# Linear attention with experts on one core: the first four chunks' loads in single pieces, the first gates in halves, one product moved to GpSimd, seven warm products fewer

## The chip, the core and the metric

The kernel runs on one core of a Trainium2 chip. Five engines work side by side, each through its own list of instructions in order: TensorE (matrix products, into PSUM), VectorE, ScalarE, GpSimd and SyncE, which here issues the loads. Sixteen DMA engines move the data. The metric is the device time of one execution in microseconds; lower is better.

## The reference

A gated linear attention feeds a mixture of eight experts, of which each token takes one. There are 4 batches, 8 heads of 48 and 768 steps, so 3072 tokens of 384 values.

```python
f = 1.0 / (1.0 + np.exp(-f_logit))
for t in range(S):
    state = f[:, :, t, :, None] * state + np.einsum('bhd,bhe->bhde', k[:, :, t], v[:, :, t])
    y[:, :, t] = np.einsum('bhd,bhde->bhe', q[:, :, t], state)
...
logits = x @ w_gate
e_idx = np.argmax(logits, axis=1)
eom = 1.0 / (1.0 + np.exp(-(x @ w_output_gate)))
for e in range(E):
    h = np.maximum(x[mask] @ w1[e], 0.0)
    out[mask] = gate_w[mask, None] * eom[mask, e, None] * (h @ w2[e])
```

## The kernel before

**Tiles.** A chunk is 128 steps of one batch, all heads: 6 chunks a batch, 24 in all, numbered t = 0 to 23 in `order` (line 462). q, k and f are laid out as 128 partitions (two heads of 48, padded to 64) by 4 groups of heads (`NP`) by 768 steps; v has the steps of a chunk on the partitions.

**What a chunk needs first** (`prep`, lines 209 to 249). ScalarE turns f into gates with a sigmoid: `s` the start values (128x4) and the first element of `p`, `f` the other 127 steps of four groups (128x508) into PSUM. VectorE forms the running product `p` with one scan over all 511 elements (`scan_p`; the four groups are cut from each other by a zero at the end of each group in the gates), then a reciprocal and the scan backwards (`scan_i`). q is multiplied by `p` (`mul_q`, GpSimd) and k by `i` (`mul_k`, on VectorE for chunks 1 and 2 and from chunk 22 on, else on GpSimd). ScalarE keeps the last column (`ends`).

**The chunk itself.** TensorE forms 16 score products (`qk`, line 266) into two PSUM tiles, of which there are two in all, so that chunk t+1 writes where chunk t was read. ScalarE copies the scores out (line 271) and GpSimd masks them (line 272); from chunk 2 on VectorE masks one half from PSUM (line 277). TensorE then turns k (line 285), turns the output of two chunks before (`x_tr`, line 347, after ScalarE's copies of line 339), multiplies q with the state (line 328) and the scores with v (line 332), and adds to the state (line 301).

**The order.** Each engine's order is that of the program text (`chain`, line 1340). The loop over t (line 510) writes chunk t's products beside the preparation of chunk t+2, and the start values of chunk t+3 from t = 3 on (line 564). Ahead of the loop stand chunks 0 and 1 (lines 499 to 501) and the gates of chunk 2 (line 502).

**The loads.** SyncE issues them in order (lines 465 to 471), `load(b, cuts)` with pieces (which tensors, first chunk, chunk behind the last). One chunk of q, k or f is 256 KiB, in rows of 512 B; two chunks in one load have rows of 1024 B. Batch 0 is followed by batch 1 in pieces of two chunks.

**Warm products.** `warm_up` runs products of zeros whose results nobody reads: `WARM` = 18 at the start (line 77), 5 that wait for chunk 0's `scan_p` and 4 for its `scan_i` (lines 503 and 504).

**After the attention** the tokens are routed, scattered by expert, and the eight experts' two layers run on TensorE to the end; none of that is touched.

Of the kernel before, what the change touches and what calls it, by code (L numbers as in the profile page):

```python
# [8 lines left out]
F32 = mybir.dt.float32  # L9
# [4 lines left out]
AF = mybir.ActivationFunctionType  # L14
ALU = mybir.AluOpType
# [6 lines left out]
C = 128  # L22
NCH = S // C
NP = H // 2
CAPS = (480, 448, 432, 416, 400, 400, 384, 376)
WARM = 18
TS = 128
NT = 4
SLOTS = NT * TS
# [18 lines left out]
T_VEC = 22  # L48
# [11 lines left out]
def behind_of(tc, d, other):  # L60

    tc.add_manual_dep(d.ins, other.ins.name,
                      mybir.DependencyInfo(mybir.DependencyClass.Sync, mybir.DependencyReason.DATA), reason="order")


def warm_up(nc, k, ps, n, tc=None, after=None):
    for i in range(n):
        d = nc.tensor.matmul(ps, k.warm[:, 0:128], k.warm, start=True, stop=True)
        if after is not None and i == 0:
            behind_of(tc, d, after)  # L70


def make_consts(nc, k, pool, prep, ps, ends):

    k.warm = pool.tile([128, 512], BF16, name="warm")
    nc.vector.memset(k.warm, 0.0)
    warm_up(nc, k, ps, WARM)

# [22 lines left out]
def more_consts(nc, pool, k, r):  # L101

    k.upper = pool.tile([128, 128], BF16, name="upper")
    nc.gpsimd.memset(k.upper, 1.0)
    nc.gpsimd.affine_select(out=k.upper, in_=k.upper, pattern=[[1, 128]], compare_op=ALU.is_gt,
                            fill=0.0, base=0, channel_multiplier=-1)
    k.ones = pool.tile([128, 128], BF16, name="ones")
    nc.gpsimd.memset(k.ones, 1.0)

    k.first = pool.tile([128, E], F32, name="first")  # L110
    nc.gpsimd.iota(out=k.first, pattern=[[-1, E]], base=E, channel_multiplier=0, allow_small_or_imprecise_dtypes=True)
    k.first_key = pool.tile([128, E], F32, name="first_key")
    nc.gpsimd.iota(out=k.first_key, pattern=[[-1 - E * N, E]], base=E, channel_multiplier=0,
                   allow_small_or_imprecise_dtypes=True)

    k.num = pool.tile([128, E], F32, name="num")
    nc.gpsimd.iota(out=k.num, pattern=[[1, E]], base=0, channel_multiplier=0, allow_small_or_imprecise_dtypes=True)
    k.slot0 = pool.tile([128, E], F32, name="slot0")
    nc.gpsimd.iota(out=k.slot0, pattern=[[N, E]], base=0, channel_multiplier=0, allow_small_or_imprecise_dtypes=True)
    k.place = pool.tile([128, E, E], F32, name="place")  # L120
    nc.gpsimd.iota(out=k.place, pattern=[[1, E], [0, E]], base=0, channel_multiplier=0,
                   allow_small_or_imprecise_dtypes=True)

    nc.gpsimd.iota(out=r.ohb[:, 0, 0, :], pattern=[[N // 128, E]], base=0, channel_multiplier=0,
                   allow_small_or_imprecise_dtypes=True)
# [16 lines left out]
def attention(ctx, tc, nc, k, kpool, rt, q01, k01, f01, q23, k23, f23, v, wg, xs_dram, r, ex):  # L142
# [11 lines left out]
    pf = done_sb.enter_context(tc.tile_pool(name="at_pre", bufs=4, side="right"))  # L154
# [4 lines left out]
    f_t = [pe.tile([128, NP, S], F32, name=f"f_t{i}") for i in range(2)]  # L159
# [10 lines left out]
    f_ps = psB.tile([128, NP, C], F32, name="f_ps")  # L170
# [13 lines left out]
    def load(b, cuts, after=None):  # L184
        i = b % 2

        def issue(out, in_):
            d = nc.sync.dma_start(out=out, in_=in_)
            if after is not None:
                behind_of(tc, d, after)  # L190
        if b not in v_t:
            v_t[b] = vp.tile([128, NCH, H * 64], F32, name="v_t")
        src = {"f": (f_t[i], f01, f23), "k": (k_t[i], k01, k23), "q": (q_t[i], q01, q23)}
        for what, c0, c1 in cuts:
            sl = slice(c0 * C, c1 * C)
            for w in what:
                if w == "v":
                    issue(out=v_t[b][:, c0:c1, :], in_=v[b, sl].rearrange("(c p) h e -> p c (h e)", p=C))
                    continue
                t, first, rest = src[w]  # L200
                if b < 2:
                    issue(out=t[:, :, sl], in_=first[b, :, :, sl].rearrange("g p s -> p g s"))
                    continue
                for g in (0, 2):
                    for par in range(2):
                        issue(out=t[64 * par:64 * par + D, g:g + 2, sl],
                              in_=rest[b - 2, 2 * g + par:2 * g + par + 3:2, :, sl].rearrange("g d s -> d g s"))

    def prep(ti):
        b, c = order[ti]  # L210
        i, sl, z = b % 2, slice(c * C, (c + 1) * C), ti % 2
        flat = lambda a: a.rearrange("p g t -> p (g t)")
        eng = nc.vector if ti in (1, 2) or ti >= T_VEC else nc.gpsimd
        d = {}

        def s():

            nc.scalar.activation(out=k.start_p[z][:, :, 0:1], in_=f_t[i][:, :, c * C:c * C + 1], func=AF.Sigmoid)  # L218
            d["p"] = pf.tile([128, NP, C], F32, name="p", bufs=3)
            nc.scalar.copy(out=d["p"][:, 0, 0:1], in_=k.start_p[z][:, 0, 0:1])  # L220

        def f():

            d["f"] = {1: f_y, 2: f_x}.get(ti, f_ps)
            nc.scalar.activation(out=d["f"][:, :, 0:C - 1], in_=f_t[i][:, :, c * C + 1:c * C + C], func=AF.Sigmoid)

        def scan_p():

            n, sp = NP * C, flat(k.start_p[z])
            d["scan_p"] = nc.vector.tensor_tensor_scan(out=flat(d["p"])[:, 1:n], data0=flat(d["f"])[:, 0:n - 1], data1=sp[:, 1:n],  # L230
                                         initial=sp[:, 0:1], op0=ALU.mult, op1=ALU.max)

        def scan_i():

            nc.vector.reciprocal(out=k.start_i[z][:, :, C - 1:C], in_=d["p"][:, :, C - 1:C])
            d["i"] = pf.tile([128, NP, C], F32, name="i", bufs=3)
            d["scan_i"] = nc.vector.tensor_tensor_scan(out=flat(d["i"])[:, ::-1], data0=flat(d["f"])[:, ::-1],  # L237
                                         data1=flat(k.start_i[z])[:, ::-1], initial=0.0, op0=ALU.mult, op1=ALU.max)

        def mul_k():  # L240
            d["mul_k"] = eng.tensor_tensor(out=k_t[i][:, :, sl], in0=k_t[i][:, :, sl], in1=d["i"], op=ALU.mult)

        def mul_q():
            nc.gpsimd.tensor_tensor(out=q_t[i][:, :, sl], in0=q_t[i][:, :, sl], in1=d["p"], op=ALU.mult)  # L244

        def ends():
            nc.scalar.copy(out=r.pend[:, ti * NP:ti * NP + NP].unsqueeze(2), in_=d["p"][:, :, C - 1:C])

        return locals()
# [4 lines left out]
    def hot(t):  # L254
        return 0 <= t < len(order)
# [206 lines left out]
    order = [(b, c) for b in range(B) for c in range(NCH)]  # L462
    last = len(order) - 1
    pre_of = [prep(t) for t in range(len(order))]
    load(0, [("f", 0, 1), ("q", 0, 2), ("f", 1, 2), ("k", 0, 2), ("f", 2, 4), ("v", 0, 1), ("qk", 2, 4)])
    nc.sync.dma_start(out=turn[:, 0::2, 2 * D:XW], in_=wg[:, 0::2, 0:2 * E])
    for i in range(2):
        nc.sync.dma_start(out=turn[64 * i:64 * i + 64, 1::2, 2 * D:XW],
                          in_=wg[64 - 64 * i:128 - 64 * i, 1::2, 0:2 * E])
    load(0, [("v", 1, 4), ("fkqv", 4, 6)])  # L470
    load(1, [("fkqv", 0, 2), ("fkqv", 2, 4), ("fkqv", 4, 6)])
    ex.empty_rows()

    def pre(t, *names):
        if hot(t):
            for nm in names:
                if nm not in done[t]:
                    done[t].add(nm)
                    pre_of[t][nm]()
# [13 lines left out]
    for g in range(2):  # L493
        for j in range(2):
            r0 = 64 * (j ^ g)
            nc.gpsimd.tensor_copy(out=turn[:, g::2, D * j:D * j + D],
                                  in_=k.ident[:, r0:r0 + D].unsqueeze(1).broadcast_to([128, 2, D]))
    more_consts(nc, kpool, k, r)
    for names in (("f", "s"), ("scan_p", "mul_q", "ends", "scan_i", "mul_k")):
        pre(0, *names)  # L500
        pre(1, *names)
    pre(2, "s", "f")
    for name, n in (("scan_p", 5), ("scan_i", 4)):
        warm_up(nc, k, one, n, tc, pre_of[0]["d"][name])

    ends, t0 = {}, 0
# [3 lines left out]
    for t in range(last + 1):  # L510
# [84 lines left out]
        if t in share:  # L595
            b, what, c = share[t]
# [823 lines left out]
```

## Time and profile before

| | us |
|---|---|
| median of 3 runs | 336.77 (335.91 to 337.01) |
| the profiled execution | 335.95 |
| its span, first to last instruction | 334.2 |
| TensorE busy in the span | 326.7 |
| first score products of chunk 0 | 9.68 |
| first score products of chunk 2 | 15.09 |

The profile is of one execution; its times count from its first instruction. A row of a timeline gives the start, the duration, the engine, the line, the operation with the tile written and the tiles read, and in brackets how long the engine had been idle and what ended that. "x16" means that 16 instructions of one kind stand together in the row.

### The profile page before, as it was taken

The numbers are of one execution on the slowest core, as the hardware profiler recorded it, in microseconds if no ns is written. First come the engines' busy times: TensorE is split into PE (matmuls) and PEld (weight loads), VectorE is DVE, ScalarE is ACT, GpSimd is POOL, SyncE is SP. The second block draws the span as 40 slices with busy tenths as digits, with TensorE's granted clock in tenths as the row PEclk, the third lists the DMA queues.
The fourth block names the chain that finished last, engine by engine and source line by source line (L and its number), as shares of the span: only waits on it lengthen the run. The fifth ranks groups of instructions, "written<-read, shape, count | busy, mean of one in ns | idle before, by whom it ended". The sixth has DMA issues, their size and how long they took to land. (4 is left out here: it accounts for less than half of the span.)

```text
span 334.2 us, 8698 instructions
## 1 busy us (share of the span) xinstructions
PE 326.7 (98%) x3002; PEld 307.9 (92%) x3002; DVE 262.6 (79%) x538; ACT 182.5 (55%) x434; POOL 144.4 (43%) x185
## 2 busy tenths in 40 slices
PE   8999999999999999999999999999999999999993
PEld 3788888889898899999999999999999999999992
DVE  6999999898999677586885985985986886989700
ACT  4777776877775762565642543452552662553610
POOL 7778789999988883031000005003104103203251
PEclk9999999999999999999999999999999999999999
DMA  7999999966666834999999399699699699593531
GB/s 241 348 355 360 303 227 275 251 180 203 195 220 216 263 140 158 239 183 348 130 301 216 54 294 316 125 263 341 137 250 328 140 234 329 156 252 115 141 121 46
DMA packets 85715, 75.15 MB, mean 225 GB/s; under 512 B 40661, under 2 KB 80278, under 8 KB 85648
## 3 DMA queue, kind: packets, MB, share of 16 engines
q1 hardware_dynamic: 82352, 64.61, 71.2%
q0 software_dynamic: 3296, 9.65, 8.2%
q8 instruction: 42, 0.69, 0.9%
q14 instruction: 25, 0.20, 0.2%
HBM read 57.83 MB, written 16.81 MB: 223 GB/s over the span
## 5 line engine op out<-in xcount | busy, mean ns | idle before, releaser
L1041 POOL DMA_INDIRECT out<-yr,dst x23 | 23.6, 1025 | 129.4 <-DMA yr<-yd 95.1
L947 PE MATMUL h_ps<-xl,w1h 128*128 128x224 f32 (+7 forms) x192 | 63.2, 329 | 0.0
L947 PE MATMUL h_ps<-xh,w1l 128*128 128x224 f32 (+7 forms) x192 | 63.1, 329 | 0.0
L947 PE MATMUL h_ps<-xh,w1h 128*128 128x224 f32 (+7 forms) x192 | 62.9, 328 | 0.0
L958 ACT ACTIVATE hh<-h_ps 128x400 fp32r<-128x400 f32 (+7 forms) x70 | 33.8, 483 | 52.1 <-PE h_ps L947 51.1
L959 DVE SCALAR_TENSOR_TENSOR hl<-h_ps,hh 128x400 fp32r<-128x400 f32 (+7 forms) x70 | 37.5, 537 | 22.8 <-ACT hh L958 22.3
L979 PE MATMUL y_ps<-hh,w2l 128*128 128x424 f32 (+5 forms) x144 | 49.0, 341 | 0.0
L979 PE MATMUL y_ps<-hl,w2h 128*128 128x424 f32 (+5 forms) x144 | 48.9, 340 | 0.0
L979 PE MATMUL y_ps<-hh,w2h 128*128 128x424 f32 (+5 forms) x144 | 48.9, 339 | 0.0
L947 PEld LDWEIGHTS h_ps<-xh,w1h 128*128 128x128 f32 x192 | 36.1, 188 | 0.2
L947 PEld LDWEIGHTS h_ps<-xh,w1l 128*128 128x128 f32 x192 | 36.1, 188 | 0.1
L947 PEld LDWEIGHTS h_ps<-xl,w1h 128*128 128x128 f32 x192 | 36.1, 188 | 0.1
L244 POOL TENSOR_TENSOR q_t<-q_t,p 128x512 f32<-128x512 f32 x24 | 30.6, 1275 | 3.4 <-DMA q_t<-in_q 1.6
L741 DVE TENSOR_TENSOR w2l<-w2r,w2h 128x768 fp32r<-128x768 f32 x31 | 29.6, 956 | 2.5 <-ACT w2h L740 0.7
L230 DVE TENSOR_TENSOR_SCAN p<-f_ps,start_p 128x511 f32<-128x511 f32 x22 | 28.0, 1274 | 2.8 <-ACT start_p L218 1.2
L266 PE MATMUL a_ps<-q_t,k_t 64*128 64x128 f32 x384 | 28.3, 285 | 0.2 <-ACT at L271 0.2
L237 DVE TENSOR_TENSOR_SCAN i<-f_ps,start_i 128x512 f32<-128x512 f32 x22 | 26.9, 1223 | 0.8
L741 DVE TENSOR_TENSOR w1l<-w1r,w1h 128x768 fp32r<-128x768 f32 x28 | 26.6, 952 | 0.9 <-ACT w1h L740 0.2
L364 POOL DMA_INDIRECT xs_dram<-xn,slot x24 | 24.1, 1006 | 7.1 <-issue 3.6
L979 PEld LDWEIGHTS y_ps<-hh,w2h 128*128 128x128 f32 x144 | 27.0, 188 | 0.1
L979 PEld LDWEIGHTS y_ps<-hl,w2h 128*128 128x128 f32 x144 | 27.0, 188 | 0.1
L979 PEld LDWEIGHTS y_ps<-hh,w2l 128*128 128x128 f32 x144 | 27.0, 188 | 0.1
(201 smaller groups left out, 736.4 us busy)
## 6 DMA issues: line engine op xcount, KB each, us to landing
w1r<-in_w SPq DMA_DIRECT2D x32, 384.0 KB, 6.2
w2r<-in_w SPq DMA_DIRECT2D x32, 384.0 KB, 5.6
v_t<-in_v SPq DMA_DIRECT2D x5, 768.0 KB, 10.7
yr<-yd SPq DMA_DIRECT2D x6, 576.0 KB, 7.8
q_t<-in_q SPq DMA_DIRECT2D x6, 512.0 KB, 8.5
k_t<-in_k SPq DMA_DIRECT2D x6, 512.0 KB, 10.5
f_t<-in_f SPq DMA_DIRECT2D x5, 512.0 KB, 7.6
xs_dram<-empty SPq DMA_DIRECT2D x6, 401.0 KB, 3.3
```

The lines of the kernel that those rows point to most:

```text
L230: d["scan_p"] = nc.vector.tensor_tensor_scan(out=flat(d["p"])[:, 1:n], data0=flat(d["f"])[:, 0:n - 1], data1=sp[:, 1:n], initial=sp[:, 0:1 ...
L237: d["scan_i"] = nc.vector.tensor_tensor_scan(out=flat(d["i"])[:, ::-1], data0=flat(d["f"])[:, ::-1], data1=flat(k.start_i[z])[:, ::-1], in ...
L244: nc.gpsimd.tensor_tensor(out=q_t[i][:, :, sl], in0=q_t[i][:, :, sl], in1=d["p"], op=ALU.mult)
L266: turns[t] = nc.tensor.matmul(aps[t][par][:, g, :], k_t[b % 2][r, g, sl], q_t[b % 2][r, g, sl], start=(g == 0), stop=(g == NP - 1))
L364: i = nc.gpsimd.indirect_dma_start(out=xs_dram, out_offset=bass.IndirectOffsetOnAxis(ap=r.slot[:, t:t + 1], axis=0), in_=xn[t // 4][:, t % ...
L741: (eng or self.nc.vector).tensor_tensor(out=flat(lo), in0=raw, in1=flat(hi.bitcast(F32)), op=ALU.subtract)
L947: nc.tensor.matmul(ps[:, 0:n], a[:, c, cs], b[:, 0:n], start=(i == 0), stop=(i == 3 * KC - 1))
L958: nc.scalar.activation(out=hi, in_=ps[:, 0:n], func=AF.Relu)
L959: nc.vector.scalar_tensor_tensor(out=lo, in0=ps[:, 0:n], scalar=0.0, in1=hi.bitcast(F32), op0=ALU.max, op1=ALU.subtract)
L979: self.nc.tensor.matmul(self.yps[d][:, 0:n], a[:, d, fs], b[:, 0:n], start=(f == 0 and i == 0), stop=(f == KF - 1 and i == 2), skip_group_ ...
L1041: self.other_rows(self.nc.gpsimd.indirect_dma_start(out=self.out, out_offset=bass.IndirectOffsetOnAxis(ap=self.k.dst[0:n, j, s:s + 1], axi ...
```

## The change

The first four chunks of batch 0 are loaded chunk by chunk, in an order written out by hand: f of chunk 0 in two loads of two head groups each, then q0, f1, k0, q1, k1, f2, q2, v0, k2, f3, the three small gate-weight loads, q3, v1, k3, and the rest of batch 0 with v in single chunks. The gates of chunk 0 are formed in two halves (`head`): ScalarE does start values and sigmoids of two groups at a time, and VectorE scans the first two groups while ScalarE works on the others. `mul_k` of chunk 1 goes from VectorE to GpSimd. The text ahead of the loop is put in a new order, in which VectorE has chunk 0's backward scan ahead of chunk 1's forward scan, as before. The warm products go from 18 + 5 + 4 to 12 + 5 + 3.

```diff
-WARM = 18
+WARM = 12
...
-        for what, c0, c1 in cuts:
+        for what, c0, c1, *gs in cuts:
             sl = slice(c0 * C, c1 * C)
+            gs = slice(*gs) if gs else slice(0, NP)
...
-                    issue(out=t[:, :, sl], in_=first[b, :, :, sl].rearrange("g p s -> p g s"))
+                    issue(out=t[:, gs, sl], in_=first[b, gs, :, sl].rearrange("g p s -> p g s"))
...
-        eng = nc.vector if ti in (1, 2) or ti >= T_VEC else nc.gpsimd
+        eng = nc.vector if ti == 2 or ti >= T_VEC else nc.gpsimd
         d = {}
+
+        def head():
+
+            d["f"] = f_ps
+            d["p"] = pf.tile([128, NP, C], F32, name="p", bufs=3)
+            sp = flat(k.start_p[z])
+            for g in (0, 2):
+                gs = slice(g, g + 2)
+                nc.scalar.activation(out=k.start_p[z][:, gs, 0:1], in_=f_t[i][:, gs, c * C:c * C + 1], func=AF.Sigmoid)
+                nc.scalar.activation(out=d["f"][:, gs, 0:C - 1], in_=f_t[i][:, gs, c * C + 1:c * C + C],
+                                     func=AF.Sigmoid)
+            nc.scalar.copy(out=d["p"][:, 0, 0:1], in_=k.start_p[z][:, 0, 0:1])
+            for a, b in ((1, 2 * C), (2 * C, NP * C)):
+                d["scan_p"] = nc.vector.tensor_tensor_scan(
+                    out=flat(d["p"])[:, a:b], data0=flat(d["f"])[:, a - 1:b - 1], data1=sp[:, a:b],
+                    initial=sp[:, 0:1], op0=ALU.mult, op1=ALU.max)
...
-    load(0, [("f", 0, 1), ("q", 0, 2), ("f", 1, 2), ("k", 0, 2), ("f", 2, 4), ("v", 0, 1), ("qk", 2, 4)])
+    load(0, [("f", 0, 1, 0, 2), ("f", 0, 1, 2, 4), ("q", 0, 1), ("f", 1, 2), ("k", 0, 1), ("qk", 1, 2), ("fq", 2, 3),
+             ("v", 0, 1), ("k", 2, 3), ("f", 3, 4)])
...
-    load(0, [("v", 1, 4), ("fkqv", 4, 6)])
+    load(0, [("q", 3, 4), ("v", 1, 2), ("k", 3, 4), ("f", 4, 6), ("v", 2, 3), ("qk", 4, 6), ("v", 3, 4), ("v", 4, 6)])
...
-    for names in (("f", "s"), ("scan_p", "mul_q", "ends", "scan_i", "mul_k")):
-        pre(0, *names)
-        pre(1, *names)
+    pre(0, "head")
+    pre(1, "f", "s")
+    pre(0, "mul_q", "ends", "scan_i", "mul_k")
+    pre(1, "scan_p", "mul_q", "ends", "scan_i", "mul_k")
     pre(2, "s", "f")
-    for name, n in (("scan_p", 5), ("scan_i", 4)):
+    for name, n in (("scan_p", 5), ("scan_i", 3)):
         warm_up(nc, k, one, n, tc, pre_of[0]["d"][name])
```

## Rows read from the trace of the kernel before

**Rows 1.** The page: TensorE's busy time, and granted clock and DMA in 40 slices.
```profile
PE 326.7 (98%) x3002; PEld 307.9 (92%) x3002; DVE 262.6 (79%) x538; ACT 182.5 (55%) x434; POOL 144.4 (43%) x185
...
PEclk9999999999999999999999999999999999999999
DMA  7999999966666834999999399699699699593531
```

**Rows 2.** Timeline of TensorE, 0 to 30 us: start, duration, group, idle before.
```profile
1.26 6.49 PE L68 MATMUL kn_ps<-warm 128*128 128x512 bf16 x18 [1.26 <-DVE warm L76]
7.58 2.11 PE L68 MATMUL one_ps<-warm 128*128 128x512 bf16 x9
9.68 1.16 PE L266 MATMUL a_ps<-q_t,k_t 64*128 64x128 f32 x16
...
11.59 1.60 PE L266 MATMUL a_ps<-q_t,k_t 64*128 64x128 f32 x16 [0.15 <-ACT at L271]
...
15.09 1.16 PE L266 MATMUL a_ps<-q_t,k_t 64*128 64x128 f32 x16
...
25.99 1.04 PE L347 MATMUL x_ps<-turn,xt 128*128 128x112 f32 x8
```

**Rows 3.** Waits of TensorE's weight loads, 14 to 99 us: total, times, longest.
```profile
PEld two_ps L328 <- DVE state L316: 0.2, 1, 0.2
...
PEld a_ps L266 <- POOL at L272: 0.2, 1, 0.2
```

**Rows 4.** Timeline of ScalarE, 0 to 30 us.
```profile
3.92 0.60 ACT L225 ACTIVATE f_ps<-f_t 128x508 f32<-128x508 f32 x1 [1.61 <-DMA f_t<-in_f]
...
9.74 0.21 ACT L218 ACTIVATE start_p<-f_t 128x4 f32<-128x4 f32 x1 [0.73 <-DMA f_t<-in_f]
...
10.09 0.59 ACT L225 ACTIVATE x_ps<-f_t 128x508 f32<-128x508 f32 x1
10.89 1.09 ACT L271 ACTIVATE at<-a_ps 128x512 f32<-128x512 f32 x2 [0.21 <-PE a_ps L266]
...
24.58 0.22 ACT L218 ACTIVATE start_p<-f_t 128x4 f32<-128x4 f32 x1 [0.27 <-DMA f_t<-in_f]
...
25.24 0.38 ACT L339 COPY xt<-one_ps 128x256 f32<-128x256 f32 x1
```

**Rows 5.** Timeline of VectorE, 0 to 30 us.
```profile
4.68 1.28 DVE L230 TENSOR_TENSOR_SCAN p<-f_ps,start_p 128x511 f32<-128x511 f32 x1 [1.20 <-ACT start_p L218]
...
6.21 1.22 DVE L237 TENSOR_TENSOR_SCAN i<-f_ps,start_i 128x512 f32<-128x512 f32 x1
...
10.29 1.12 DVE L241 TENSOR_TENSOR k_t<-k_t,i 128x512 f32<-128x512 f32 x1
...
14.11 0.69 DVE L241 TENSOR_TENSOR k_t<-k_t,i 128x512 f32<-128x512 f32 x1
```

**Rows 6.** Timeline of GpSimd, 0 to 30 us.
```profile
5.56 0.13 POOL L124 IOTA ohb<- 128x8 bf16 x1
...
8.36 1.27 POOL L241 TENSOR_TENSOR k_t<-k_t,i 128x512 f32<-128x512 f32 x1 [0.99 <-DMA k_t<-in_k]
...
11.56 1.22 POOL L272 TENSOR_SCALAR_AFFINE_SELECT at<-at 128x512 f32<-128x512 f32 x2 [0.70 <-ACT at L271]
...
21.74 1.27 POOL L244 TENSOR_TENSOR q_t<-q_t,p 128x512 f32<-128x512 f32 x1 [1.65 <-DMA q_t<-in_q]
```

**Rows 7.** DMA packets of 2.0 to 2.8, 4.8 to 5.3 (512 B), 6.5 to 8.0 (1024 B).
```profile
DMA packets 332, 0.17 MB, mean 212 GB/s; under 512 B 0, under 2 KB 332, under 8 KB 332
...
DMA packets 323, 0.17 MB, mean 336 GB/s; under 512 B 5, under 2 KB 323, under 8 KB 323
...
DMA packets 539, 0.54 MB, mean 357 GB/s; under 512 B 16, under 2 KB 539, under 8 KB 539
```

**Rows 8.** Timeline of SyncE: issues of loads.
```profile
0.80 0.46 SPq L188 DMA_DIRECT2D f_t<-in_f  x1
```

**Rows 9.** Stretch after TensorE's last product: busy PE, PEld, DVE, ACT, POOL; clock, DMA.
```profile
328.70:334.20 5.50, 0.00 (x0) 0.00 (x0) 0.00 (x0) 0.57 (x1) 1.03 (x1) 0.97 0.13 34
```

## The prediction

> **What bounds the kernel now.** I read the page first: TensorE is busy 98% of the span and its granted clock is 9 tenths or more in every slice [rows 1]. A busy TensorE says little, since matmuls overlap, so the next view was its timeline. From chunk 2's score products at 15.09 on, one group starts where the one before ends, about 4.5 us a chunk [rows 2]; the waits of its weight loads from 14 to 99 us, beside issue, are four of 0.2 us [rows 3]. So the work from 15 us on is a solid block: what moves its start moves the end one to one, and so does any hole cut into it. Only the front can give time back. It is a relay: f lands, ScalarE makes gates (3.92), VectorE scans (4.68, 6.21), GpSimd multiplies k (8.36), TensorE starts at 9.68 [rows 2, 4 to 6]. The second reading is the queue of loads: it is full already (357 GB/s against 336 where rows of 512 B run [rows 7]), and ScalarE still waits 0.27 us for f of batch 1 at 24.58, GpSimd 1.65 for q at 21.74 [rows 4, 6]. The front and the loads both hold the block's start.
>
> **The gates in halves.** The whole f of chunk 0 is in at about 3.85. At the 212 GB/s of that stretch [rows 7] half of it (131 KB) takes 0.6 us, so the first half is in at 3.25; the second at 3.85, or up to 0.3 later for the extra issue (one takes 0.46 us [rows 8]). ScalarE's half gates cost about 0.38 us (its 256-element copy [rows 4]) and the start values 0.1 to 0.2, so they end at 3.9 and 4.45 and the half scans, 0.64 each (half of 1.28 [rows 5]), at 4.55 and 5.2. Before it was 4.68 + 1.28 = 5.96: 0.75 earlier, 0.45 if the second half is late. The backward scan ends at 5.2 + 0.2 + 1.22 = 6.65 instead of 7.43. GpSimd is busy with constants until 5.56 + 0.13 [rows 6], so q of chunk 0 is multiplied from 5.8 to 7.07.
>
> **Loads in order of need.** Up to k of chunk 0, 1 MiB is now ahead instead of 1.5. At 357 GB/s that is 1.47 us, less some 0.1 for two loads turned into 512-byte rows: k lands at 6.9 instead of 8.25, and its product, behind q's, runs from 7.1 to 8.35. Chunk 0's score products start near 8.4 instead of 9.68. But that start is not what sets the block. Chunk 1's 16 products take 1.60 us instead of 1.16 [rows 2]: they wait for ScalarE, whose two copies out of PSUM run from 10.89 to 11.98 [rows 4], so their true start is 12.0. ScalarE works in order, and ahead of those copies stand chunk 2's gates, which wait for chunk 2's f (9.74, then 10.09 + 0.59 [rows 4]). That f has 1.75 MiB ahead of and with it instead of 2: 0.73 us less; five loads that were 1024-byte rows or longer pay for 512 bytes (0.05 each, below) and some extra issues: it lands at 9.25 to 9.55. Gates done, the copies start at 10.2 to 10.5 instead of 10.89: 0.4 to 0.7 earlier, and I take 0.55.
>
> **Chunk 1's k on GpSimd.** It leaves VectorE (1.12 us at 10.29 [rows 5]) and goes behind GpSimd's k of chunk 0 and q of chunk 1 (1.27 each [rows 6]): 8.35 + 1.25 = 9.6, then 9.75 to 11.0, when VectorE had it done at 11.41. Queued behind it are chunk 0's two masks (11.56 before [rows 6]), now from 11.0 on. It hides under ScalarE's copies, which end at 11.4; without that cover it would cost what it exceeds them by. VectorE, 1.12 us freer, starts chunk 2's scan as its gates are done, at 10.35, and has its k multiplied by 14.0 rather than 14.80 [rows 5]: no longer last. So chunk 2's products start 0.55 earlier, at 14.5.
>
> **Seven warm products fewer.** Before, they end as chunk 0's products begin, 7.58 + 2.11 = 9.69 [rows 2]; left as they were they would hold the new 8.4 back. Twelve cold ones and eight more end near 8.0. The idle 0.4 us before 8.4 costs nothing: after TensorE's last product the granted clock still averaged 0.97 over 328.70 to 334.20 [rows 9].
>
> **The price of the short rows.** Ten pieces of 256 KiB (q and k of four chunks, f of two) change from rows of 1024 B to 512 B. Lower bound, from the stretches where each runs undisturbed: 2.62 MB at 336 GB/s is 7.80 us, at 357 it is 7.34 [rows 7], so 0.46 us. Upper bound, the 212 GB/s of the start, where the queue was still filling: 12.4 us, so 5.0. I take near the lower end, since the queue is full by then, plus 0.25 for eight more issues on SP and for the three small gate-weight loads taking slots among shorter ones (not shown; 0 to 0.5): 0.7 us. The bytes ahead of f of batch 1 are the same as before, so it lands at 24.56 + 0.7 = 25.25.
> Who waits for that: ScalarE, in order, at 24.58. Behind it stand the copies of chunk 2's output (the second 25.24 + 0.38 = 25.62), which TensorE turns at 25.99 [rows 2, 4]. That turn's first two products need the first copy alone, so it could have begun at about 25.45: 0.54 us of slack. The block therefore moves by the larger of (minus the front's gain) and (the delay of the load minus 0.54). With 0.55 and 0.7 that is max(-0.55, +0.16) = **+0.16 us**: the front's gain is given back, in one hole before that turn. The q of chunk 4 (GpSimd at 21.74) goes ahead of its k and of v of chunk 3, so it is not later. The later loads of batch 1 are waited for by nobody in the trace, and DMA eases after 67 us [rows 1].
>
> Against the profiled execution, 335.95 us (span 334.2), that is 336.1. The median of the runs is 336.77, 0.82 above it, so 336.95, which I round to 337.0. A measurement of this kernel can tell about 0.3%, 1.0 us, from no change.
>
> **Rivals.**
> (A) The forecast: gain given back at the load of batch 1's f. Front 0.4 to 0.7, delay 0.4 to 1.1: -0.15 to +0.6, so 336.6 to 337.4. Chance 0.46.
> (B) Short rows cost nothing. Then f of batch 1 lands at 24.56 as before and the block keeps min(0.55, 0.54): 336.25. For it: packets of 512 B run with the engines fully busy too [rows 7]. Against it: 336 is 6% under 357. The Trainium skill, page "DMA: Bandwidth & Descriptors", section "Specifications", puts the least transfer for full rate at 512 B, by which this is the case; the trace agrees to within those 6%. The same page's "Rules for kernel authors" asks for at least 1 MiB in one DMA, by which all of these loads, before and after, are short. Chance 0.24.
> (C) Slower: the loads, not TensorE, set the block. It decides from a delay of about 1.55 us (f of batch 1 after 26.1), when the hole passes 1.0 us; at 2.0 us the turn starts at 24.56 + 2.0 + 0.89 = 27.45 instead of 25.99: 338.2. For it: the DMA engines are full in the second slice already [rows 1], and the far bound is 5.0. Against it: mid-stream rows show 0.46. Chance 0.18.
> (D) More comes through: chunk 2's f by 8.8, so that copies start with chunk 0's products' end (9.55) and only GpSimd's k at 11.0 holds chunk 1: 1.0 us, if batch 1's f comes 0.5 earlier too: 335.75. Chance 0.09.
> (E) The halves don't overlap, or the idle before 8.4 grows to microseconds and the clock falls to 1.2 GHz. The first alone changes nothing, since chunk 2's f sets the pace; the second would run about 5 us of products at half rate, as the first 18 warm ones ran (6.49 us, against 2.11 for nine [rows 2]), and lose 2.5: 339.3. Chance 0.03.
>
> **Chances and range.** Faster by over 0.3%: D and the best of B, 0.14. Slower: most of C, E and a tail of A, 0.20. Within: 0.66. The range from 336.0 to 338.2 leaves out D and half of C.
>
> **What would show it.** Right: first score products at 8.2 to 8.7, chunk 2's at 14.4 to 14.7; ScalarE idle 1 to 2 us before the start values of chunk 6, and TensorE idle before chunk 2's turn. Wrong: ScalarE's copies at 10.9 or later (front gains nothing); no wait on f of batch 1 (B or D); a turn after 27 (C); GpSimd's k of chunk 1 ending after the copies (the moved product costs); a granted clock under 1.0 before 15 us (E).

## The result and the profile after

The change made the kernel slower: 338.78 us (338.11 to 339.13) against 336.62 us (335.91 to 337.01) for the kernel before, six runs each, a ratio of 1.0058 with a 95% interval of 1.0033 to 1.0082, so 2 us. The forecast was 337.0 us, its range ended at 338.2 us, and "slower" had a chance of 0.20. The profiled execution took 338.61 us, with a span of 336.9. Two single executions far from all others, of 639 us in experiment 2 and of 1789 us in experiment 8, are left out of the ratios below.

The page of the kernel after, TensorE's busy time and the slices of granted clock and DMA, says almost nothing of this (compare [rows 1]): TensorE is as busy for as long, its clock as high, and the DMA row of the first 67 us (eight slices) reads the same.

```profile
PE 326.7 (97%) x2995; PEld 307.9 (91%) x2995; DVE 261.8 (78%) x538; ACT 181.6 (54%) x436; POOL 144.6 (43%) x186
...
PEclk9999999999999999999999999999999999999998
DMA  7999999966666924999998399699889789693521
```

The timelines say it. ScalarE's, kernel after, 0 to 30 us (columns as in [rows 4]):

```profile
3.32 0.37 ACT L225 ACTIVATE f_ps<-f_t 128x254 f32<-128x254 f32 x1
...
3.83 0.37 ACT L225 ACTIVATE f_ps<-f_t 128x254 f32<-128x254 f32 x1
...
10.28 0.21 ACT L235 ACTIVATE start_p<-f_t 128x4 f32<-128x4 f32 x1 [1.78 <-DMA f_t<-in_f]
...
11.14 1.06 ACT L288 ACTIVATE at<-a_ps 128x512 f32<-128x512 f32 x2
...
18.77 0.21 ACT L235 ACTIVATE start_p<-f_t 128x4 f32<-128x4 f32 x1 [1.25 <-DMA f_t<-in_f]
...
26.62 0.21 ACT L235 ACTIVATE start_p<-f_t 128x4 f32<-128x4 f32 x1 [1.39 <-DMA f_t<-in_f]
...
27.28 0.38 ACT L356 COPY xt<-one_ps 128x256 f32<-128x256 f32 x1
```

The gates of chunk 0 are early, as meant (sigmoids from 3.32 to 4.20 where one ran from 3.92 to 4.52 in [rows 4]). Then ScalarE waits for f three times: for chunk 2's until 10.28 (9.74 before), for that of chunks 4 and 5 until 18.77 (17.38 before, without a wait worth a row), and for that of batch 1 until 26.62 (24.58 before). The third is 2.04 us late.

TensorE's timeline of the kernel after, 0 to 30 us (the groups of [rows 2]):

```profile
9.01 1.16 PE L283 MATMUL a_ps<-q_t,k_t 64*128 64x128 f32 x16 [0.29 <-POOL k_t L258]
...
11.87 1.55 PE L283 MATMUL a_ps<-q_t,k_t 64*128 64x128 f32 x16 [1.11 <-ACT at L288]
...
15.31 1.16 PE L283 MATMUL a_ps<-q_t,k_t 64*128 64x128 f32 x16
...
21.79 1.15 PE L364 MATMUL x_ps<-turn,xt 128*128 128x112 f32 x8 [0.17 <-ACT xn L372]
...
27.44 1.20 PE L364 MATMUL x_ps<-turn,xt 128*128 128x112 f32 x8 [0.51 <-ACT xt L356]
```

Chunk 0's score products start 0.67 us earlier than before, chunk 2's 0.22 later (15.31 against 15.09): the early start is gone before it reaches the solid block. The turn of chunk 2's output starts at 27.44 instead of 25.99, after a hole. TensorE's weight loads had four waits of 0.2 us in [rows 3], beside issue; now the longest are these (waits of weight loads, 14 to 99 us: total, times, longest):

```profile
PEld x_ps L364 <- ACT xt L356: 0.8, 1, 0.8
PEld two_ps L345 <- DVE state L333: 0.4, 1, 0.4
PEld x_ps L364 <- ACT xn L372: 0.4, 1, 0.4
```

VectorE's timeline of the kernel after shows whose chain had no room, and in its first row that the halves did not overlap:

```profile
4.23 1.39 DVE L229 TENSOR_TENSOR_SCAN p<-f_ps,start_p 128x255 f32<-128x255 f32 x2 [0.75 <-ACT f_ps L225]
...
19.74 1.28 DVE L247 TENSOR_TENSOR_SCAN p<-f_ps,start_p 128x511 f32<-128x511 f32 x1 [0.69 <-ACT f_ps L242]
...
27.69 0.36 DVE L332 TENSOR_TENSOR misc<-one_ps,state 128x192 f32<-128x192 f32 x1 [1.25 <-ACT xt L356]
...
28.36 1.27 DVE L247 TENSOR_TENSOR_SCAN p<-f_ps,start_p 128x511 f32<-128x511 f32 x1
```

The first row holds both half scans. The first of them starts at 4.23, just behind the end of ScalarE's second sigmoid (3.83 + 0.37 = 4.20), and not behind the first (3.69), so VectorE did not scan two groups while ScalarE worked on the others; the row gives that wait as 0.75 us.

The third row is VectorE's addition to the state: it waits 1.25 us for the same copies of chunk 2's output as TensorE's turn does, copies that stand on ScalarE behind the late start values (26.62). The scan of chunk 6 comes next in VectorE's order. Chunk 4's scan (19.74) starts 0.91 us later than before, chunk 6's (28.36) 2.03 later, nearly the whole delay of its f. Against the kernel before, the starts of TensorE's score products lie later by 0.28 us at chunk 1, 0.77 at 4, 1.60 at 5 to 7, and 2.20 from chunk 8 to chunk 23. That is the 2 us of the result. (In this one profile another 0.45 us comes up at 115 us, where the routing ends.)

### The profile page after: what moved, and what is told of

Its sections match the earlier page's. It is cut to its first block, busy times and chain, and to the rows that moved or that the text cites. A ratio compares the mean times of both kernels' runs of the same rounds, so it can differ in the third digit from the quotient of the medians.

```text
span 336.9 us, 8698 instructions
## 1 busy us (share of the span) xinstructions
PE 326.7 (97%) x2995; PEld 307.9 (91%) x2995; DVE 261.8 (78%) x538; ACT 181.6 (54%) x436; POOL 144.6 (43%) x186
## 5 line engine op out<-in xcount | busy, mean ns | idle before, releaser
L247 DVE TENSOR_TENSOR_SCAN p<-f_ps,start_p 128x511 f32<-128x511 f32 x21 | 26.8, 1274 | 2.8 <-ACT f_ps L242 1.6
L258 POOL TENSOR_TENSOR k_t<-k_t,i 128x512 f32<-128x512 f32 x21 | 26.9, 1281 | 3.6 <-DVE i L254 1.3
L283 PEld LDWEIGHTS a_ps<-q_t,k_t 64*128 64x128 f32 x384 | 23.9, 187 | 3.6 <-POOL k_t L258 2.1
```

What stands on the lines that cost most here:

```text
L283: turns[t] = nc.tensor.matmul(aps[t][par][:, g, :], k_t[b % 2][r, g, sl], q_t[b % 2][r, g, sl], start=(g == 0), stop=(g == NP - 1))
```

## The experiments

After the trace the theory was this: f of chunks 4 and 5 and f of batch 1 come late because of the short rows, and VectorE, which has no slack, hands the delay on. Its rivals: the halves or the moved product cost the time; the number of loads does and not their rows; TensorE's slack swallows the delay and something else is the cause. Every ratio is against runs of the kernel before on the same chip. "Later" and "earlier" are starts in the trace against the trace of the kernel before.

**1. The change with the old loads.** The two lines of loads of batch 0 are put back; the halves, the moved product and the warm products stay.

```diff
-    load(0, [("f", 0, 1, 0, 2), ("f", 0, 1, 2, 4), ("q", 0, 1), ("f", 1, 2), ("k", 0, 1), ("qk", 1, 2), ("fq", 2, 3),
-             ("v", 0, 1), ("k", 2, 3), ("f", 3, 4)])
+    load(0, [("f", 0, 1), ("q", 0, 2), ("f", 1, 2), ("k", 0, 2), ("f", 2, 4), ("v", 0, 1), ("qk", 2, 4)])
...
-    load(0, [("q", 3, 4), ("v", 1, 2), ("k", 3, 4), ("f", 4, 6), ("v", 2, 3), ("qk", 4, 6), ("v", 3, 4), ("v", 4, 6)])
+    load(0, [("v", 1, 4), ("fkqv", 4, 6)])
```

> The changed kernel with the loads of the kernel before; everything else of the change stays (gates in halves, k of chunk 1 on GpSimd, new text order, 20 warm products). Theory L (the loads alone cost the time): start values of chunk 4 at 17.4 us and of chunk 6 at 24.6 us as in the kernel before, no idle TensorE before the turn of chunk 2's output, chunk 2's score products at 15.0 to 15.3, whole time 336.4 to 337.0. Rival F (the new front costs part of it: k of chunk 1 queued on GpSimd behind two products): chunk 2's score products after 15.8 us and a time of 337.7 or more.

Measured: 336.83 us against 336.31, ratio 1.0033 (1.0002 to 1.0063). In the trace ScalarE's start values of chunk 2 stand at 9.75 again and the two later waits for f are gone; TensorE lies up to 0.18 later up to chunk 7 and 0.3 later after it. So the loads carry most of the loss, and what is left of the change brings no gain, but a small loss, whose interval only just leaves out no change. Its place in the trace: chunk 1's products start at 12.14, and what released them was k of chunk 1, now GpSimd's fourth product, no longer ScalarE.

```profile
10.82 1.26 POOL L258 TENSOR_TENSOR k_t<-k_t,i 128x512 f32<-128x512 f32 x1
...
12.14 1.16 PE L283 MATMUL a_ps<-q_t,k_t 64*128 64x128 f32 x16 [0.70 <-POOL k_t L258]
```

**2. The kernel before with the new loads.** The edit of experiment 1 the other way round, in the kernel before; with it the cut by groups in `load`, nothing else of the change.

```diff
-        for what, c0, c1 in cuts:
+        for what, c0, c1, *gs in cuts:
...
+            gs = slice(*gs) if gs else slice(0, NP)
...
-    load(0, [("v", 1, 4), ("fkqv", 4, 6)])
+    load(0, [("q", 3, 4), ("v", 1, 2), ("k", 3, 4), ("f", 4, 6), ("v", 2, 3), ("qk", 4, 6), ("v", 3, 4), ("v", 4, 6)])
```

> The kernel before with the loads of the changed kernel alone. Theory L: the start values of chunk 6 wait for their f until 26.3 to 26.9 us, the turn of chunk 2's output starts at 27.2 to 27.7, whole time 338.4 to 339.2. Rival F: half of the loss or less, 337.7 or under.

Measured: 338.12 us against 336.31, ratio 1.0041 (1.0027 to 1.0055). The time is a little under the expected range. The profiled execution was a longer one, 339.06 us; there ScalarE waited for f of batch 1 until 27.81 (2.25 us idle) and TensorE lay 2.98 us later from chunk 8 on. The loads alone make a loss of this size. With the same loads, f of batch 1 was in at 26.60 in the kernel after and at 27.79 here, so a landing read from one trace can be off by a microsecond.

**3 and 4. Rows or number of loads.** Both kernels are the one before with each long load of the first eight cut in two, so that they issue as many loads; one cuts by head groups (rows stay 1024 B), the other by chunks (rows 512 B). The bytes and the order are the same. The line that goes, then the one by groups, then the one by chunks in its place:

```diff
-    load(0, [("f", 0, 1), ("q", 0, 2), ("f", 1, 2), ("k", 0, 2), ("f", 2, 4), ("v", 0, 1), ("qk", 2, 4)])
...
+    load(0, [("f", 0, 1), ("q", 0, 2, 0, 2), ("q", 0, 2, 2, 4), ("f", 1, 2), ("k", 0, 2, 0, 2), ("k", 0, 2, 2, 4),
+             ("f", 2, 4, 0, 2), ("f", 2, 4, 2, 4), ("v", 0, 1), ("q", 2, 4, 0, 2), ("q", 2, 4, 2, 4),
+             ("k", 2, 4, 0, 2), ("k", 2, 4, 2, 4)])
...
+    load(0, [("f", 0, 1), ("q", 0, 1), ("q", 1, 2), ("f", 1, 2), ("k", 0, 1), ("k", 1, 2),
+             ("f", 2, 3), ("f", 3, 4), ("v", 0, 1), ("q", 2, 3), ("q", 3, 4),
+             ("k", 2, 3), ("k", 3, 4)])
```

> The kernel before, its order of loads, with each of the five two-chunk loads of q, k and f of chunks 0 to 3 cut into two by head groups: as many loads of 256 KiB as after the change, but rows still of 1024 B. Theory rows (short rows cost): f of batch 1 lands within 0.3 us of 24.56, time 336.4 to 337.0. Rival slots (more and smaller loads in flight leave DMA engines idle): f of batch 1 0.5 us or more later, as far as in the run with the same loads cut by chunks.

> The same as the run cut by head groups, cut by chunks instead: the same number and size of loads in the same places, rows of 512 B. Theory rows: f of batch 1 lands 1.2 to 1.8 us later than 24.56 (ten pieces by 0.12 to 0.18 us), the turn of chunk 2's output 0.6 to 1.2 us later, time 337.2 to 338.0. Rival slots: no difference from the run cut by head groups.

Measured: by groups 336.81 us, ratio 1.0009 (0.9986 to 1.0032), and f of batch 1 in at 24.76, 0.2 us after the kernel before. By chunks 339.52 us, ratio 1.011 (1.0055 to 1.0164), and f of batch 1 in at 26.49, 1.93 us late (landing times here and below are the last completion that the trace records for that load). By this load the number of loads costs 0.2 us and the length of rows 1.73, and the times agree in kind: 0.5 us, not clear of noise, against 3.2.

In the kernel cut by chunks it is not f of batch 1 that holds the block, though. f of chunks 4 and 5 was in at 20.62, 3.26 us after the kernel before (by groups at 18.20, 0.84 after), ScalarE waited 3.06 us for it, TensorE lay 2.64 later from chunk 4 on, and nothing waited for f of batch 1. The forecast of 337.2 to 338.0 had followed f of batch 1 alone. ScalarE in that kernel:

```profile
20.64 0.21 ACT L219 ACTIVATE start_p<-f_t 128x4 f32<-128x4 f32 x1 [3.06 <-DMA f_t<-in_f]
```

How the rows do so is in the table of stretches (stretch, its length, busy time of PE, PEld, DVE, ACT and POOL, granted clock, share of the DMA engines, GB/s): first the kernel before, then by groups, by chunks, and the kernel after.

```profile
5.00:13.00 8.00, 7.85 (x55) 4.48 (x53) 7.69 (x10) 3.87 (x12) 5.90 (x13) 1.00 1.10 340
13.00:14.00 1.00, 1.00 (x12) 0.72 (x12) 1.00 (x1) 0.78 (x2) 1.00 (x1) 1.00 1.02 347
14.00:15.00 1.00, 1.00 (x32) 1.00 (x28) 0.76 (x2) 0.91 (x4) 0.09 (x2) 1.00 1.04 376
15.00:16.00 1.00, 1.00 (x24) 0.94 (x18) 0.72 (x1) 1.00 (x4) 1.00 (x2) 1.00 1.10 354
```
```profile
5.00:13.00 8.00, 6.14 (x38) 3.54 (x36) 7.51 (x8) 2.82 (x10) 4.48 (x11) 0.88 1.06 331
13.00:14.00 1.00, 1.00 (x7) 0.78 (x7) 0.93 (x3) 1.00 (x3) 1.00 (x2) 0.50 0.79 194
14.00:15.00 1.00, 1.00 (x15) 0.90 (x11) 0.98 (x1) 0.01 (x1) 1.00 (x2) 0.74 1.06 406
```
```profile
5.00:13.00 8.00, 7.32 (x53) 4.18 (x52) 6.77 (x8) 3.61 (x11) 5.61 (x12) 1.00 1.14 299
13.00:14.00 1.00, 1.00 (x13) 0.71 (x9) 0.93 (x3) 0.68 (x2) 0.92 (x2) 1.00 1.08 229
14.00:15.00 1.00, 1.00 (x21) 1.00 (x22) 0.89 (x2) 0.91 (x5) 0.43 (x1) 1.00 0.62 125
15.00:16.00 1.00, 0.95 (x26) 0.85 (x24) 0.78 (x2) 1.00 (x3) 0.51 (x1) 1.00 0.62 220
```
```profile
5.00:13.00 8.00, 6.59 (x46) 3.69 (x45) 6.29 (x9) 3.68 (x12) 6.88 (x14) 1.00 1.10 284
13.00:14.00 1.00, 1.00 (x12) 0.71 (x11) 1.00 (x1) 0.55 (x2) 1.00 (x2) 1.00 1.14 315
14.00:15.00 1.00, 1.00 (x25) 1.00 (x26) 0.77 (x1) 0.91 (x5) 0.32 (x2) 1.00 0.86 254
15.00:16.00 1.00, 1.00 (x30) 0.95 (x26) 0.48 (x1) 1.00 (x3) 1.00 (x2) 1.00 0.75 192
```

Two things are to be seen. From 5 to 13 us the engines are full in all four (a share over 1), and what they move falls from 331 GB/s with rows of mostly 1024 B to 299 with mostly 512 B at the same number of loads: 8 us x 32 GB/s = 0.26 MB, 0.8 us. And behind the short rows the queue runs dry, 0.62 of the engines busy from 14 to 16 us by chunks, 0.86 and 0.75 in the kernel after. SyncE's timeline has the issue of the load that comes behind the gate weights (before, by groups, by chunks):

```profile
8.90 0.59 SPq L188 DMA_DIRECT2D v_t<-in_v  x1
```
```profile
11.30 0.50 SPq L188 DMA_DIRECT2D v_t<-in_v  x1
```
```profile
13.12 0.59 SPq L188 DMA_DIRECT2D v_t<-in_v  x1
```

Where it goes out at 8.90 the engines stay full; at 11.30 there is a dip of 1 us, at 13.12 one of 2. That the late issue makes the dip fits these three, but it is not the time of the issue alone: in the kernel after that load goes out at 10.91 and the queue is dry at 14 to 16, while in experiment 7 one goes out at 10.94 and the engines stay full there (1.12 and 1.21). There a load of 512 KiB in rows of 1024 B stands in that place, in the kernel after one of 256 KiB. What makes the dip stays open between the issue and the bytes behind it. For the kernel after the same sum is: from 5 to 13 us (340 - 284) x 8 = 0.45 MB, from 13 to 16 us (347 + 376 + 354) - (315 + 254 + 192) = 0.32 MB; at 350 GB/s 1.3 + 0.9 = 2.2 us, where f of batch 1 was measured 2.04 late.

The Trainium skill, page "DMA: Bandwidth & Descriptors", section "Bandwidth" (on why small descriptors are slow), gives each packet some three cycles on top of one for every 32 bytes. For one of 1024 B that is 35 against 38 in two of 512 B, an estimate of 9% from that page; 331 to 299 is 10%, so the trace agrees, as near as windows with some rows of other lengths can tell.

**5. Delay f of batch 1 alone.** In the kernel before, k of batch 1 goes ahead of its f.

```diff
-    load(1, [("fkqv", 0, 2), ("fkqv", 2, 4), ("fkqv", 4, 6)])
+    load(1, [("kfqv", 0, 2), ("fkqv", 2, 4), ("fkqv", 4, 6)])
```

> The kernel before with one pair of loads exchanged: batch 1's k of its first two chunks goes ahead of its f, so f lands one load later, near 26.0 us instead of 24.56, and nothing else of the loads before it moves. Theory V (VectorE's chain of scans has no slack there, and its shift reaches TensorE in the end): the scan of chunk 6 starts 1.3 to 1.5 us later than 26.33, and from chunk 9 on TensorE's score products are as late, 1.2 to 1.5 us; time 337.6 to 338.0. Rival T (the prediction's sum: TensorE's turn of chunk 2's output is what waits, with 0.54 us of slack, and VectorE catches up): 0.8 to 0.95 us later from chunk 5 to the end; time 337.1 to 337.3.

Measured: 337.13 us against 336.48, ratio 1.0025 (1.0015 to 1.0036). f lands 1.68 us later than before; ScalarE, VectorE and TensorE of this kernel:

```profile
26.26 0.21 ACT L218 ACTIVATE start_p<-f_t 128x4 f32<-128x4 f32 x1 [1.84 <-DMA f_t<-in_f]
```
```profile
28.00 1.27 DVE L230 TENSOR_TENSOR_SCAN p<-f_ps,start_p 128x511 f32<-128x511 f32 x1
```
```profile
27.07 1.20 PE L347 MATMUL x_ps<-turn,xt 128*128 128x112 f32 x8 [0.67 <-ACT xt L339]
```

VectorE's scan of chunk 6 comes 1.67 us later, the turn 1.08 later, and TensorE lies 1.24 later at chunks 5 to 7 and 1.44 later from chunk 8 to the end (0.11 of it is there from chunk 0 on). So the slack stands where the prediction saw it: 1.68 less 0.54 is 1.14, and the turn follows it. VectorE takes the delay whole, and from chunk 8 on that adds 0.20 to TensorE's. By the trace theory V is right in that VectorE has no slack, but what this adds beyond the turn is small.

The time, 337.13, lies in the range given for rival T (337.1 to 337.3) and under that of theory V. It does not decide: between the two profiled executions the difference is 1.43 us (337.38 against 335.95), between the medians 0.65, since this kernel's profiled execution lay 0.25 over its median and that of the kernel before 0.53 under the median here.

**6. f of batch 1 early again, in the change.** It goes ahead of v of chunks 4 and 5.

```diff
-    load(0, [("q", 3, 4), ("v", 1, 2), ("k", 3, 4), ("f", 4, 6), ("v", 2, 3), ("qk", 4, 6), ("v", 3, 4), ("v", 4, 6)])
-    load(1, [("fkqv", 0, 2), ("fkqv", 2, 4), ("fkqv", 4, 6)])
+    load(0, [("q", 3, 4), ("v", 1, 2), ("k", 3, 4), ("f", 4, 6), ("v", 2, 3), ("qk", 4, 6), ("v", 3, 4)])
+    load(1, [("f", 0, 2)])
+    load(0, [("v", 4, 6)])
+    load(1, [("kqv", 0, 2), ("fkqv", 2, 4), ("fkqv", 4, 6)])
```

> The changed kernel with f of batch 1's first two chunks loaded ahead of v of batch 0's last two. Theory V: f lands 1.3 to 1.5 us earlier, near 25.2; VectorE's shift against the kernel before stays at the 0.9 us that it has from chunk 4 (late f of chunks 4 and 5), TensorE's end is 0.8 to 1.2 us behind the kernel before: time 337.2 to 337.6. Rival T: only the hole before the turn of chunk 2's output closes (0.8 us of the changed kernel's 2.2), time 337.9 to 338.1.

Measured: 337.29 us against 336.48, ratio 1.0028 (1.0014 to 1.0042). f lands at 25.30 and the hole ahead of the turn of chunk 2 is gone, but f of chunks 4 and 5 still makes ScalarE wait until 19.24: VectorE lies 1.39 later from chunk 4 on, TensorE 1.24, then 1.49 from chunk 8. The time lies in the range of theory V (337.2 to 337.6) and under that of T. One late load is removed and the other sets the block.

**7. Both f loads early, in the change.** Against experiment 6, f of chunks 4 and 5 goes right behind the gate weights as well.

```diff
-    load(0, [("q", 3, 4), ("v", 1, 2), ("k", 3, 4), ("f", 4, 6), ("v", 2, 3), ("qk", 4, 6), ("v", 3, 4)])
+    load(0, [("f", 4, 6), ("q", 3, 4), ("k", 3, 4), ("v", 1, 2), ("v", 2, 3), ("qk", 4, 6), ("v", 3, 4)])
```

> The changed kernel with both late f loads moved up: f of chunks 4 and 5 right behind the gate weights, f of batch 1's first two chunks ahead of v of batch 0's last two. Theory V (all of the loss beyond 0.25 us comes through these two loads): VectorE's shift at most 0.4 us from chunk 3 on, time 336.4 to 337.0. Rival: q, k or v of chunks 3 to 5, now later, hold the block in their place: a new wait on one of them of 0.5 us or more and a time over 337.3.

Measured: 336.78 us against 336.48, ratio 1.0011 (0.9996 to 1.0026). ScalarE waits for no f between chunk 2's and chunk 8's, which now comes late:

```profile
33.36 0.21 ACT L235 ACTIVATE start_p<-f_t 128x4 f32<-128x4 f32 x1 [0.84 <-DMA f_t<-in_f]
```

TensorE lies 0.18 us later up to chunk 7 and 0.73 from chunk 8 on. With both f loads in time the loss is gone to within what can be measured; the short rows, the late q (GpSimd's first product of batch 1 at 30.57) and all the rest are still there. These two loads carry the loss.

**8 and 9. One part each, with the old loads.** Eight has only k of chunk 1 on GpSimd, nine only the gates in halves (with the order of the front that goes with them; that is experiment 1 without the moved product and with all warm products). The line of eight:

```diff
-        eng = nc.vector if ti in (1, 2) or ti >= T_VEC else nc.gpsimd
+        eng = nc.vector if ti == 2 or ti >= T_VEC else nc.gpsimd
```

> The kernel before with one edit: k of chunk 1 multiplied by GpSimd instead of VectorE. With all of the change but its loads (the run with the old loads), TensorE's products lay 0.1 to 0.2 us later from chunk 1 to 7 and 0.3 later from chunk 8 on, and VectorE's scan of chunk 8 began 0.48 us after the event that released it instead of 0.09. Theory K (the moved product is the cause of the first part): k of chunk 1 ends near 12.1 on GpSimd, 0.1 after ScalarE's copies at 11.98, so chunk 1's products truly start 0.1 later, TensorE lies 0.1 to 0.2 later from there, scan of chunk 8 begins 0.09 after its event as before; time 0.1 to 0.2 over before. Theory G (the moved product also brings the gap at chunk 8): 0.48 there, TensorE 0.3 later from chunk 8 on; time 0.3 over. Theory N (neither): TensorE within 0.05 of before throughout; time as before. All three lie within about 0.3 us of before: the trace tells them apart, the time does not.

> The kernel before with one part of the change: f of chunk 0 loaded in two halves, its gates and scan in two halves (and the front's order that goes with it), all other loads, warm products and k of chunk 1 as before. Theory H (halves bring the gap at chunk 8): scan p of chunk 0 done at 5.5 to 5.7 instead of 5.96, chunk 0's products still at 9.7 because of k's landing, TensorE as before to chunk 7, VectorE's scan of chunk 8 0.48 us after its event and TensorE about 0.3 later from there; time 0.2 to 0.4 over before. Theory G (the moved product brings it): 0.09 there, TensorE as before throughout; time as before. If the gains of the halves were to come through (theory F), chunk 2's products would start 0.3 earlier, near 14.8, and the time would be 0.3 under before; what speaks against it is ScalarE's wait for chunk 2's f at 9.74.

Measured: 337.72 and 337.34 us against 337.83, ratios 0.9994 (0.9963 to 1.0025) and 0.9998 (0.9975 to 1.0021). In eight's profiled execution f of chunk 2 came 0.49 late by itself; TensorE lay 0.66 later at chunk 2, so some 0.17 is the moved product's, an estimate by subtraction (GpSimd's k ends at 12.57, ScalarE's copies at 12.46), and 0.05 of it was left from chunk 4 on. In nine, TensorE is 0.14 earlier at chunk 2 (f of chunk 2 came 0.14 earlier) and 0.02 later from chunk 4 on: the halves give nothing. Its forward product was done at 6.34, not at 5.5 to 5.7 and 0.38 later than before: here too the first half scan (4.95) started behind ScalarE's second sigmoid (4.92). And neither brings the gap at chunk 8; both theories that gave it to one part fall.

**10 and 11. What brings the gap at chunk 8.** Ten is the kernel before with only the seven warm products fewer, eleven is experiment 1 with these put back. The lines of ten, which eleven has the other way round:

```diff
-WARM = 18
+WARM = 12
...
-    for name, n in (("scan_p", 5), ("scan_i", 4)):
+    for name, n in (("scan_p", 5), ("scan_i", 3)):
```

> The kernel before with seven warm products fewer and nothing else. Theory W (the shorter run of warm products, which alone is left of the change, brings the 0.39 us at chunk 8): VectorE's scan of chunk 8 begins 0.48 us after the event that released it instead of 0.09, and TensorE lies 0.3 later from chunk 8 on. Theory P (the gap needs the halves and the moved product together): 0.09, and all as before; chunk 0's products at 9.7 with 1.5 us of idle TensorE ahead of them and no fall of the granted clock.

> The change with the loads of before and with the seven warm products put back, so the halves and the moved product together. Theory W: VectorE's scan of chunk 8 begins 0.09 us after its event, TensorE 0.1 to 0.2 later than before throughout (the moved product's price). Theory P: 0.48 after its event, and TensorE about 0.3 later than before from chunk 8 on.

Measured in one execution of each: 338.07 and 339.22 us, the kernel before 338.57; single times this close tell nothing apart. In ten, k of chunk 0 landed late and chunk 0's products started at 10.49, not at 9.7. The gap is read most simply as the time from chunk 7's to chunk 8's forward scan on VectorE; here the kernel before, then eleven:

```profile
30.26 1.28 DVE L230 TENSOR_TENSOR_SCAN p<-f_ps,start_p 128x511 f32<-128x511 f32 x1
...
34.77 1.27 DVE L230 TENSOR_TENSOR_SCAN p<-f_ps,start_p 128x511 f32<-128x511 f32 x1
```
```profile
31.92 1.28 DVE L247 TENSOR_TENSOR_SCAN p<-f_ps,start_p 128x511 f32<-128x511 f32 x1
...
36.83 1.28 DVE L247 TENSOR_TENSOR_SCAN p<-f_ps,start_p 128x511 f32<-128x511 f32 x1 [0.31 <-ACT at L288]
```

It is 4.51 us before, 4.51 in eight, 4.50 in nine and ten, and 4.89 to 4.91 in the kernel after, in 1, 6 and eleven. (In 7 it is 5.20: 0.31 more, with the wait for chunk 8's f.) So neither part has it alone, the warm products have no share in it, and the halves and the moved product together bring 0.39 us. The row names a copy of ScalarE (of `at`), but in 1, 6, 7, eleven and the kernel after the idle is 0.3 us each time while the named instruction ended anywhere from 0.06 to 0.30 us before the scan, which speaks against it; by what means the pair does it stays open.

## Why the prediction was wrong, step by step

**The price of the short rows** is the term that failed by most. It was taken at 0.7 us, as 0.46 for the rows, from two short windows of the kernel before (336 and 357 GB/s, [rows 7]), and 0.25 for issues. Measured: f of batch 1 2.04 us late. Over 8 us of such rows the queue moved 284 to 299 GB/s, not 336, and the item "not shown, 0 to 0.5" was a dry queue of 0.9 us. The window of 336 was half a microsecond long, [rows 7]'s 0.17 MB. The rule from the Trainium skill, page "DMA: Bandwidth & Descriptors", section "Specifications", that 512 B are enough for the full rate, on which rival B leaned, is contradicted by 331 against 299 GB/s at the same number of loads; the measurement decides.

**The slack at chunk 2's turn** was TensorE's and was there (the first copy was done 0.54 us before TensorE got to it, [rows 2, 4]), and the turn followed the sum: f 2.04 late, the turn 1.45. But the prediction asked only who waits at the turn. VectorE's addition to the state waits for the same copies, with no slack, and the scan of chunk 6 stands behind it; experiment 5 shows 1.67 of 1.68 us going through VectorE and 0.20 more reaching TensorE from chunk 8 on. By the prediction's own sum, 0.7 without slack gives 337.5, and 2.04 with the slack 336.77 + 1.5 = 338.3: the price weighs more than the slack.

**A late load that was not in the sum.** f of chunks 4 and 5 was in at 17.36 before and used at 17.38: no wait, so no row, and so it was not listed. It came 1.39 us later. Experiment 6 shows that alone it sets the block 1.24 us back.

**The front's gain.** Of its steps, the overlap of the halves failed: the first half scan was to start at 3.9, when half the gates were done, and started at 4.23, behind both sigmoids. The forward product was done at 5.62 instead of 5.96, 0.34 earlier (0.45 was the low end), and in experiment 9, with the old loads, 0.38 later than before, so the gain was the earlier f's and not the halves'. What makes VectorE wait for the second sigmoid was not tried. The moved product went as worked out: GpSimd's k of chunk 1 ended at 11.40, under ScalarE's copies, which ended at 12.20. Chunk 0's products started at 9.01, not 8.4, since k landed at 7.56, not 6.9. The step that decided was rightly named, chunk 2's f, but that landed at 10.26 instead of 9.25 to 9.55: at 284 GB/s (5 to 13 us) the smaller number of bytes ahead of it bought nothing. The copies went from 10.89 to 11.14, and the sign "copies at 10.9 or later, the front gains nothing" is what is seen. Even with the old loads the gain stayed out (experiments 1 and 9), for the same reason.

**The rivals.** C held: "the loads, not TensorE, set the block", at "2.0 us" the turn at 27.45 and the time 338.2; the turn stands at 27.44. That a delay moves the turn so was understood; that the example of 2.0 us is so near to the measured 2.04 is luck. It had 0.18 because its price was measured against the mid-stream rows. Its time fell 0.6 us short, since it moved the turn alone (1.45): the score products behind it lie 1.60 later, and from chunk 8 on 2.20, with 0.2 of VectorE's delay and the 0.39 us there, which no row of the kernel before could show. A's signs (hole ahead of the turn, idle before chunk 6's start values) are there as well, three times as large. Of E, the first half came, the halves did not overlap, and it changed nothing at chunk 2, as it said; the second did not: the granted clock is full from 8 us on, and no use of the seven warm products is seen (experiment 10, one execution: 2.05 us of idle TensorE before chunk 0's products at full clock). Its price was misread: by [rows 2] the first 18 warm products took 0.36 us each and the nine 0.23, not half the rate, and the granted clock reads 9 tenths or more over both [rows 1].

## What to carry to other kernels

When loads are cut smaller, price them by the longest stretch of such rows that can be found, not by a window of half a microsecond, and ask whether the issuing engine still runs ahead of the queue. For every load that comes later, list all readers, those that today find it just in time too: a wait that is not there yet has no row, so the list has to come from landing against first use. A step cut in two overlaps only if the second engine waits for the first half alone; look at what ended its wait. Slack belongs to one path; the load's delay goes through whichever path has none.

## What was not expected of the hardware

- Rows of 512 B against 1024 B at the same number of loads: 299 against 331 GB/s over 8 us, with the sixteen engines full in both (experiments 4 and 3).
- A load cut in two by groups was not in sooner as a whole: of k of chunks 0 and 1 the first half ended at 7.78 us and the second at 9.12 in experiment 3, the uncut load at 8.22 in the kernel before.
- In the first 100 us of all thirteen traces TensorE's granted clock fell once, in the profiled execution of experiment 3, from 11.1 to 14.5 us, to 0.50 (1.2 GHz), shortly after an idle of 1.86 us ahead of chunk 0's products; in that execution TensorE lay 1.8 to 1.9 us later than before from chunk 2 on. In experiment 10 an idle of 2.05 us at the same place was followed by full clock. TensorE's timeline in experiment 3, and its stretch with the lower clock:

```profile
10.60 1.65 PE L267 MATMUL a_ps<-q_t,k_t 64*128 64x128 f32 x16 [1.86 <-POOL k_t L242]
```
```profile
11.10:14.50 3.40, 3.40 (x27) 2.85 (x27) 3.33 (x4) 2.23 (x6) 2.20 (x4) 0.50 1.04 293
```

- The 0.39 us at chunk 8, which two edits of the first 12 us bring together and neither alone, without a wait that the profile names.
